# Attention and two MLPs on one core: first scatters on two queues, row tiles of 110, four buffers for evicted values, first activations split during attention

## The chip, the core and the metric

The kernel runs on one core of a Trainium2 chip. The metric is device time in microseconds (us) of one execution, as a median over several runs. Matmuls run on PE (TensorE), the other arithmetic on DVE (VectorE), ACT (ScalarE) and POOL (GpSimd). SP (SyncE) issues nearly all transfers; their packets are carried by the core's 16 DMA engines.

## The reference

Attention over 4 batches, 12 heads, 448 rows and 64 dimensions, with the heads mixed before and after the softmax; then two MLPs on the 1792 x 768 result.

```python
scores = scale * np.matmul(q, k.transpose(0, 1, 3, 2))
scores = np.einsum('bhij,hg->bgij', scores, w_pre)
scores = scores - np.max(scores, axis=-1, keepdims=True)
attn = np.exp(scores)
attn = attn / (np.sum(attn, axis=-1, keepdims=True) + 1e-09)
attn = np.einsum('bhij,hg->bgij', attn, w_post)
attn_out = np.matmul(attn, v)          # -> x: 1792 x 768
h = 1 / (1 + np.exp(-(x @ w_gate))) * (x @ w_val)    # 768 -> 1536
x = h @ w_out                                         # 1536 -> 768
h = np.maximum(x @ w_in, 0.0)                         # 768 -> 2048
out = h * h @ w_out2                                  # 2048 -> 768
```

## The kernel before

**Tiles and steps.** row_tiles (L31) cuts a batch's 448 rows into four tiles of 120, 120, 120 and 88 rows, and each tile is cut into groups of 10 rows (the last one of a batch has 8): 12, 12, 12 and 9 groups, 45 a batch, 180 in all. Two tiles make a chunk (240 and 208 columns). The loop of attention takes one group a step: premix (L182) multiplies a group's 120 (row, head) lines with the first head mixer, maximum (L190) and exponent (L198) make the softmax on DVE and ACT, normal (L209) scales the second mixer by the sums on POOL, and postmix (L224), three steps later, applies it and transposes. When a chunk's groups are through, values (L253) multiplies it by v for two heads at a time, six units a chunk.

**The scatter.** The scores of a tile come out with one row per partition, for one head at a time (L156, pairs of heads p, outputs o). ACT copies them to a buffer e (L166; DVE at L164 for the second output in the first tile), and SP scatters e into g (L170), where one partition holds one (row, head) and premix can contract over heads. If a tile of isz rows has ng whole groups and a rest, an output takes two transfers: rest partitions-groups of ng + 1 rows, and GI - rest of ng rows. A tile of 120 rows is one transfer of 10 x 12 rows of 448 floats (1792 bytes each); the tile of 88 rows is two, 8 x 9 and 2 x 8. The twelve outputs of tile n are scattered during the steps of tile n - 1: pairs p = 0 to 5, one pair a step, the last at most LA = 3 steps before the first premix of tile n, which needs all twelve. g has two buffers, e has four pairs.

**What SP's queue holds beside it.** In program order: k of the next batch (L129, one after each pair in the last tile of a batch), q of the next tile (L137), v (L243), the stores of evicted values (xs from xo, L269), and what the MLP asks for. An xo buffer is filled by ACT (L268) from PSUM; it comes from the pool pv, which has two buffers, so the third copy waits for the first store.

**The MLP beside attention.** The MLP is a generator, advanced by attention: in the last EARLY = 64 steps every third step gives it one piece ("yield 1"), and after the last scores every step two ("yield 2"); beyond the last premix three. Its list `early` there loads the first weight tiles (w_raw, 768 KB each, L422) and splits them into high and low parts over several stages. Then x_steps loads the attention output back (xr, L530) and splits it (xh on ACT, L546; xl on POOL or DVE), for chunks c of 0 and 1 (batches 0 and 1), six tiles each. Its buffers xr come from a pool of two, and the split results stand in the pool px, which is opened only after the buffers of the scores are closed. From 566 us on PE runs the MLP's matmuls alone (L612).

**Order.** The program is scheduled by hand: the order in which the loop issues instructions is the order on each engine. PE, ACT, DVE, POOL and SP each go through their own in order.

Of the kernel before, what the change touches and what calls it, by code (L numbers as in the profile page):

```python
# [7 lines left out]
F32 = mybir.dt.float32  # L8
# [8 lines left out]
P = 128  # L17
# [5 lines left out]
NA = 9  # L23
MW, PW, VW, SW, STEP = 0.76, 0.82, 1.66, 1.04, 2.55
KB = 10
EARLY = 64
EM = 2
EACH = (1, 2, 2)


def row_tiles(S):  # L31

    n = -(-S // (4 * GI)) * GI
    cuts = [t * n for t in range(4)] + [S]
    return list(zip(cuts, cuts[1:]))

# [6 lines left out]
def attention(tc, q, k, v, w_pre, w_post, xs, B, H, S, D):  # L43
# [31 lines left out]
    with ExitStack() as ctx, ExitStack() as mid, ExitStack() as left:  # L75
        kw = dict(side="right")
        one = ctx.enter_context(tc.tile_pool(name="a_one", bufs=1, **kw))
        pv = ctx.enter_context(tc.tile_pool(name="a_v", bufs=2, **kw))
        pp = ctx.enter_context(tc.tile_pool(name="a_p", bufs=1, **kw))
        pa = mid.enter_context(tc.tile_pool(name="a_a", bufs=NA, **kw))  # L80
        pg = mid.enter_context(tc.tile_pool(name="a_g", bufs=2, **kw))
# [60 lines left out]
        def scores(n, p):  # L142

            b, i0, isz = tiles[n]
            if p == 0:
                g_t[n] = pg.tile([KM, GT, S], F32, tag="g", name="g")
            kt = k_t.pop((b, p)) if i0 + isz == S else k_t[b, p]
            ps = [
                ps_b.tile([P, S], F32, tag="b", name="ps_s")
                if n == 0 and p % 2  # L150
                else ps_q.tile([P, S], F32, tag="q", name="ps_s")
                for _ in range(2)
            ]
            for o in range(2):
                r = slice(o * D, (o + 1) * D)
                nc.tensor.matmul(  # L156
                    ps[o][:isz], lhsT=q_t[n][r, p, :isz], rhs=kt[r], start=True, stop=True
                )
            e = p4.tile([IM, 2, S], F32, tag="e", name="e")
            ng, rest = divmod(isz, GI)  # L160
            to = g_t[n].rearrange("(r h) g j -> h r g j", h=H)
            for o in range(2):
                if n == 0 and o:
                    nc.vector.tensor_copy(e[:isz, o], ps[o][:isz])  # L164
                else:
                    nc.scalar.copy(e[:isz, o], ps[o][:isz])  # L166
                for r0, r1, g in ((0, rest, ng + 1), (rest, GI, ng)):
                    if r0 < r1:
                        e0 = r0 * (ng + 1)
                        nc.sync.dma_start(  # L170
                            out=to[2 * p + o, r0:r1, :g], in_=e[e0 : e0 + (r1 - r0) * g, o]
                        )


# [89 lines left out]
        def valued(c, h, ps):  # L264
            b, i0, i1 = chunks[c][:3]
            w = i1 - i0
            xo = pv.tile([P, CM], F32, tag="xo", name="xo")
            nc.scalar.copy(xo[:, :w], ps[:, :w])  # L268
            nc.sync.dma_start(out=xs[b][h * D : (h + 2) * D, i0:i1], in_=xo[:, :w])  # L269

# [41 lines left out]
            load_next(k_load, k_order)  # L312
            load_next(k_load, k_order)
        masks()
        q_load(1)
        for p in range(NP):
            scores(0, p)
        mixers()
        for _ in range(2):
            load_next(v_load, v_order)  # L320
        for _ in range(KB - NP):
            load_next(k_load, k_order)
        for s in range(NG + 30):
            if s < NG:
                premix(s)
            flush()
            if s < NG:
                maximum(s)
            if 1 <= s <= NG:
                exponent(s - 1)  # L330
            if 2 <= s < NG + 2:
                normal(s - 2)
            left_over = STEP - MW
            ready = front and front[0][0] <= s
            if ready and due(s):
                next_scores()
                ready, left_over = False, left_over - SW
            fresh = None
            while bpos < len(back) and (left_over > 0.5 or s >= NG):
                f, cost, *x = back[bpos]  # L340
                if f is postmix:
                    if x[0] > s - LAG:
                        break
                    fresh = groups[x[0]][3]
                elif x[0] == fresh:
                    if s < NG:
                        break
                    flush()
                if len(pending) > 3:
                    flush()  # L350
                f(*x)
                if f is values and (x[1] + 2) % HV == 0:
                    pending.append((load_next, v_load, v_order))
                bpos += 1
                left_over -= cost
                if f is postmix and x[0] == NG - 1:
                    flush()
                    mid.close()
                if s >= NG:
                    yield 3 if bpos == len(back) or back[bpos][0] is values else 2  # L360
            if ready and left_over > 0.4:
                next_scores()
            if not front and not closed:
                left.close()
                closed = True
            if NG - EARLY <= s < NG:
                if closed:
                    yield 2
                elif s % 3 == 0:
                    yield 1  # L370
# [3 lines left out]
def mlp(tc, xs, wg, wv, wo, wi2, wo2, out, DM, DF1, DF2):  # L374
# [12 lines left out]
    with ExitStack() as ctx:  # L387
# [5 lines left out]
        pf = pool("m_f", 2, side="left")  # L393
        p1 = pool("m_1", 1, side="left")
        pw3 = pool("m_w3", 3, side="left")
        pw = pool("m_w", 3, side="left")
        dram = pool("m_dram", 1, space=DRAM)
        yield 1

# [126 lines left out]
        xr = {}  # L526

        def x_load(hf, c, i):
            xr[c, i] = pf.tile([P, N], F32, tag="xr", name="xr")
            nc.sync.dma_start(out=xr[c, i], in_=xs[hf * NC + c][i * P : (i + 1) * P, :])  # L530

        def halves(p, tag, src):
# [8 lines left out]

        def x_split(hf, c, i):
            t = xr.pop((c, i))
            hi = px.tile([P, N], F32R, tag="xh", name="xh")
            lo = px.tile([P, N], F32R, tag="xl", name="xl")
            nc.scalar.copy(hi, t)  # L546
            (nc.vector if hf or i % 2 else nc.gpsimd).tensor_tensor(
                out=lo, in0=t, in1=hi.bitcast(F32), op=ALU.subtract
            )
            xt[c, i] = (hi, lo)  # L550

        def x_steps(hf):
            if hf * NC < NX:
                todo = [(c, i) for c in range(NC) for i in range(KD)]
                for n in range(len(todo) + 2):
                    if n >= 2:
                        x_split(hf, *todo[n - 2])
# [3 lines left out]
                        yield  # L561


        steps = x_steps(0)

        early = [0, 0, 1, 2, 0, 1, 3, 0, 2, 4, 1, 3, 2, 4, 3, 1]
        for n, k in enumerate(early):
            advance(k)
            yield 1 if n + 1 < len(early) else 2
        px = pool("m_x", KD * NC, side="left")  # L570
        for n, _ in enumerate(steps):
            if n in (4, 10):
                advance(5)
            if n in (7, 13):
                advance(6)
            if n == 8:
                advance(0)
            yield 2 if n < 14 else 3
        yield 3
        pe = pool("m_e", 3, side="left")  # L580
        ph0 = pool("m_h0", EM * NC, side="left")
# [81 lines left out]
        for hf in range(NX // NC):  # L663
# [24 lines left out]
                w_used()  # L688

            x2 = {}  # L690
            long(K1, KD, g, lambda c, m, ps: to(x2, (c, m), px, "x", ps))

            hh = {}
            while (NC - 1, KD - 1) not in x2:
# [5 lines left out]
                    product(ps, wt, x2, c, then=squared(hh, c, m, ps))  # L700
                w_used()

            todo = iter(x_steps(hf + 1))
            long(K2, KD, hh, lambda c, m, ps: store(hf, c, m, ps), todo)
            for _ in todo:
                pass
# [63 lines left out]
```

## Time and profile before

| | us |
|---|---|
| median of 3 runs | 1523.88 (1523.6 to 1529.14) |
| profiled execution, its time | 1531.59 |
| profiled execution, its span | 1529.9 |
| PE busy in the span | 1491.3 (97%), 38.6 idle |
| DVE, ACT, POOL busy | 765.1 (50%), 537.8 (35%), 508.0 (33%) |
| L612, the MLP's matmuls, at the end of the span | from 566.00, 960.35 us, 4714 of them |

PE is the engine that is nearly always busy, so the views to read are those of PE's idle time and of PE's order: what it waited for, the time from one premix to the next (a step), and which transfer or engine released it. A row of the timeline gives start and length in us, the engine (SPq is SP's queue of issues), the line, and in brackets the idle time before it with what ended it. PEclk is the clock that was granted to PE, 1.00 for 2.4 GHz and 0.50 for 1.2 GHz. The share of the DMA engines is a mean over 16.

### The profile page before, as it was taken

The page shows a single profiled execution, that of the slowest core. Times are in us where ns is not written, and L with a number is a line of the kernel's source. Part 1 is how long each engine was busy: PE and PEld are TensorE (multiplying, and loading weights), DVE is VectorE, ACT ScalarE, POOL GpSimd, SP SyncE. Part 2 cuts the span into 40 slices and gives each one's busy share as a digit, 9 for nine tenths or more (in the row PEclk, how much of TensorE's full clock was granted, in tenths as well). Part 3 has the DMA queues.
Part 4 walks back from the last instruction along what each step waited for, and adds up shares of the span by engine and source line. Part 5 has one row for each costly group of instructions (what it writes and reads, how often), then busy time and mean ns, then how long its engine had stood idle before and what let it go on. Part 6 is the DMA issues. An engine that isn't in the chain of part 4 may idle for free.

```text
span 1529.9 us, 21163 instructions
## 1 busy us (share of the span) xinstructions
PE 1491.3 (97%) x7848; PEld 1210.1 (79%) x7848; DVE 765.1 (50%) x1275; ACT 537.8 (35%) x1102; POOL 508.0 (33%) x403
## 2 busy tenths in 40 slices
PE   5999999999999899999999999999999999999999
PEld 2555656646555689999999999999999999999998
DVE  2645546546474478777889998921111101333000
ACT  3544444444344333333234443322222212333111
POOL 0222222221223346455555555532222222223221
PEclk8999999999999999999999999999999999999999
DMA  6354454445534344444444446632111111112221
GB/s 216 109 151 131 125 147 141 125 137 160 160 99 152 94 158 176 165 156 158 173 159 161 157 160 203 216 122 62 43 61 54 61 42 59 55 52 60 77 71 42
DMA packets 79531, 185.42 MB, mean 121 GB/s; under 512 B 11204, under 2 KB 48452, under 8 KB 79428
## 3 DMA queue, kind: packets, MB, share of 16 engines
q1 hardware_dynamic: 79428, 184.07, 37.5%
q8 instruction: 62, 1.02, 0.3%
q14 instruction: 41, 0.34, 0.1%
HBM read 107.75 MB, written 37.75 MB: 95 GB/s over the span
## 4 chain that ended last, share of the span: by engine, by line
PE 63%; DMA 0%; DVE 0%; POOL 0%; issue 0%; ACT 0%; ACTq 0%; DVEq 0%; SPq 0%; POOLq 0%
PE ps L612 63%; DMA w_raw<-in_wv 0%; POOL w L472 0%; POOL wl L485 0%; DVE w_t L454 0%; ACT w_f L432 0%; DVE w_f L461 0%; DVE w L441 0%; DVE w_t L438 0%; ACT o L644 0%; DVE ps L630 0%; DVEq L441 0%; ACTq L644 0%; SPq L422 0%; POOLq L472 0%
## 5 line engine op out<-in xcount | busy, mean ns | idle before, releaser
L485 POOL TENSOR_TENSOR wl<-w,wh 128x768 fp32r<-128x768 f32 (+1 forms) x140 | 259.4, 1855 | 544.7 <-ACT wh L479 538.6
L612 PE MATMUL ps<-xh,wl 128*128 128x448 f32 x960 | 351.1, 366 | 1.2 <-POOL wl L485 1.2
L612 PE MATMUL ps<-xh,wh 128*128 128x448 f32 x960 | 351.4, 366 | 0.0
L612 PE MATMUL ps<-xl,wh 128*128 128x448 f32 x960 | 351.1, 366 | 0.0
L612 PE MATMUL ps<-hl,wh 128*128 128x448 f32 x672 | 246.8, 367 | 0.0
L612 PE MATMUL ps<-hh,wl 128*128 128x448 f32 x672 | 246.8, 367 | 0.0
L612 PE MATMUL ps<-hh,wh 128*128 128x448 f32 x672 | 246.6, 367 | 0.0
L209 POOL TENSOR_SCALAR wn<-wq,sm 120x120 f32<-120x120 f32 x180 | 107.2, 596 | 386.4 <-DVE sm L207 249.7
L224 PEld LDWEIGHTS ps_p<-wn,a 120*112 120x112 f32 (+1 forms) x1440 | 164.6, 178 | 74.5 <-issue 46.4
L182 PE MATMUL ps_m<-g,wp 120*120 120x448 f32 x360 | 177.0, 574 | 22.4 <-DMA g<-e 11.9
L612 PEld LDWEIGHTS ps<-xh,wl 128*128 128x128 f32 x960 | 180.6, 188 | 16.2 <-POOL wl L485 1.8
L190 DVE TENSOR_REDUCE nm<-ps_m 120x1 f32<-120x448 f32 x180 | 112.3, 624 | 161.0 <-PE ps_m L182 152.3
L612 PEld LDWEIGHTS ps<-xh,wh 128*128 128x128 f32 x960 | 180.6, 188 | 15.4 <-issue 0.9
L612 PEld LDWEIGHTS ps<-xl,wh 128*128 128x128 f32 x960 | 180.6, 188 | 14.4
L224 PE MATMUL ps_p<-wn,a 120*112 120x120 f32 (+1 forms) x1440 | 177.4, 271 | 3.5 <-POOL wn L209 3.2
L472 POOL TENSOR_TENSOR w<-w,w_f 128x768 f32<-128x768 f32 (+1 forms) x70 | 135.3, 1933 | 60.1 <-DVE w_f L461 60.1
L236 DVE COPY ap<-ps_p 112x480 f32<-112x480 f32 x180 | 117.5, 654 | 49.8 <-PE ps_p L224 48.9
L198 ACT ACTIVATE a<-ps_m,nm 120x448 f32<-120x448 f32 x180 | 115.4, 641 | 74.7 <-DVE sm L204 63.0
L612 PEld LDWEIGHTS ps<-hh,wh 128*128 128x128 f32 x672 | 126.1, 188 | 11.7
L612 PEld LDWEIGHTS ps<-hl,wh 128*128 128x128 f32 x672 | 126.1, 188 | 11.6
L612 PEld LDWEIGHTS ps<-hh,wl 128*128 128x128 f32 x672 | 126.1, 188 | 11.6
L166 ACT COPY e<-ps_s 120x448 f32<-120x448 f32 (+1 forms) x186 | 90.0, 533 | 128.2 <-PE ps_s L156 107.9
(39 smaller groups left out, 1291.5 us busy)
## 6 DMA issues: line engine op xcount, KB each, us to landing
g<-e SPq DMA_DIRECT2D x144, 210.0 KB
ws<-w SPq DMA_DIRECT2D x58, 384.0 KB
w<-ws SPq DMA_DIRECT2D x58, 384.0 KB
w_raw<-in_wo SPq DMA_DIRECT2D x18, 768.0 KB
w_raw<-in_wi SPq DMA_DIRECT2D x16, 768.0 KB
vraw<-in_v SPq DMA_DIRECT2D x24, 448.0 KB
w_raw<-in_wg SPq DMA_DIRECT2D x12, 768.0 KB
w_raw<-in_wv SPq DMA_DIRECT2D x12, 768.0 KB
```

Of the source, the lines that this page charges most:

```text
L166: nc.scalar.copy(e[:isz, o], ps[o][:isz])
L182: nc.tensor.matmul(ps[:kk], lhsT=w[:kk, :kk], rhs=g_t[n][:kk, r0 // GI], start=True, stop=True)
L190: nc.vector.tensor_reduce(out=nm[:kk], in_=ps[:kk], op=ALU.max, axis=AX.X, negate=True)
L198: nc.scalar.activation(a[:kk], ps[:kk], AF.Exp, bias=nm[:kk], accum_out=sm[:kk])
L209: nc.gpsimd.tensor_scalar(out=wn[:kk], in0=wq[:kk], scalar1=sm[:kk], scalar2=None, op0=ALU.mult)
L224: nc.tensor.matmul(ps[:JP, jt], lhsT=a[:kk, jt * JP : (jt + 1) * JP], rhs=wn[:kk].rearrange("p g i -> p (g i)"), start=True, stop=True,)
L236: nc.vector.tensor_copy(ap[c][:, :, :, g0 - i0 : g0 - i0 + rows], ps[:JP, :, :, :rows])
L472: nc.gpsimd.tensor_tensor(out=x[:, s], in0=x[:, s], in1=fs.pop(n)[:, s], op=ALU.add)
L485: nc.gpsimd.tensor_tensor(out=lo[:, s], in0=w32.pop(n)[:, s], in1=h[:, s].bitcast(F32), op=ALU.subtract)
L612: nc.tensor.matmul(ps, lhsT=a, rhs=x, start=first and n == 0, stop=last and n == total - 1)
```

## The change

- row_tiles rounds the tile down: 110, 110, 110 and 118 rows, groups 11, 11, 11, 12 (45 a batch as before), chunks of 220 and 228 columns. An output's scatter is 10 x 11 in the first three tiles, and 8 x 12 with 2 x 11 in the last.
- In the first tile the e copies of pairs 4 and 5 go to buffers of the pool of activations, which are free at that time, and four of the twelve scatters (second outputs of pairs 1, 3, 4, 5) are issued by ACT.
- The load of q for the second tile, the first two of v and four of k are moved: q behind the first scatters, v to steps 4 and 6, k to steps 8 to 11.
- xo has a pool of its own with four buffers.
- EARLY is 112. x_steps is called for chunk 0 first, every third step from step 69 on, with three xr buffers and a px pool for chunk 0 opened at the start; the list `early` follows behind it, so that w_raw falls to steps 105, 108 and 126 (before: 117, 120 and 138). The pool of rounded weights (pw) and the px pool for chunk 1 are opened where the buffers of scores are closed, and chunk 1 is split there.

```diff
-EARLY = 64
+EARLY = 112
...
 def row_tiles(S):
 
-    n = -(-S // (4 * GI)) * GI
+    n = S // (4 * GI) * GI
...
         pv = ctx.enter_context(tc.tile_pool(name="a_v", bufs=2, **kw))
+        po = ctx.enter_context(tc.tile_pool(name="a_o", bufs=4, **kw))
...
-            e = p4.tile([IM, 2, S], F32, tag="e", name="e")
+            if n == 0 and p >= 4:
+                e = [pa.tile([IM, S], F32, tag="a", name="e0") for _ in range(2)]
+            else:
+                t = p4.tile([IM, 2, S], F32, tag="e", name="e")
+                e = [t[:, o] for o in range(2)]
...
-                    nc.scalar.copy(e[:isz, o], ps[o][:isz])
+                    nc.scalar.copy(e[o][:isz], ps[o][:isz])
+                queue = nc.scalar if n == 0 and o and p in (1, 3, 4, 5) else nc.sync
                 for r0, r1, g in ((0, rest, ng + 1), (rest, GI, ng)):
                     if r0 < r1:
                         e0 = r0 * (ng + 1)
-                        nc.sync.dma_start(
-                            out=to[2 * p + o, r0:r1, :g], in_=e[e0 : e0 + (r1 - r0) * g, o]
+                        queue.dma_start(
+                            out=to[2 * p + o, r0:r1, :g], in_=e[o][e0 : e0 + (r1 - r0) * g]
                         )
...
-            xo = pv.tile([P, CM], F32, tag="xo", name="xo")
+            xo = po.tile([P, CM], F32, tag="xo", name="xo")
...
         masks()
-        q_load(1)
         for p in range(NP):
             scores(0, p)
         mixers()
-        for _ in range(2):
-            load_next(v_load, v_order)
-        for _ in range(KB - NP):
-            load_next(k_load, k_order)
+        q_load(1)
         for s in range(NG + 30):
             if s < NG:
                 premix(s)
             flush()
             if s < NG:
                 maximum(s)
+            if s in (4, 6):
+                load_next(v_load, v_order)
+            if 8 <= s < 8 + KB - NP:
+                load_next(k_load, k_order)
...
-        pw = pool("m_w", 3, side="left")
+        px = [pool("m_x0", KD, side="left")]
+        pxr = pool("m_xr", 3, side="left")
...
-            xr[c, i] = pf.tile([P, N], F32, tag="xr", name="xr")
+            xr[c, i] = pxr.tile([P, N], F32, tag="xr", name="xr")
...
-        def x_steps(hf):
+        def x_steps(hf, chunks):
             if hf * NC < NX:
-                todo = [(c, i) for c in range(NC) for i in range(KD)]
+                todo = [(c, i) for c in chunks for i in range(KD)]
...
-        steps = x_steps(0)
+        for _ in x_steps(0, [0]):
+            yield 1
 
         early = [0, 0, 1, 2, 0, 1, 3, 0, 2, 4, 1, 3, 2, 4, 3, 1]
         for n, k in enumerate(early):
             advance(k)
             yield 1 if n + 1 < len(early) else 2
-        px = pool("m_x", KD * NC, side="left")
-        for n, _ in enumerate(steps):
-            if n in (4, 10):
+        pw = pool("m_w", 3, side="left")
+        px.append(pool("m_x1", KD, side="left"))
+        for n, _ in enumerate(x_steps(0, [1])):
+            if n in (2, 6):
                 advance(5)
-            if n in (7, 13):
+            if n in (4, 8):
                 advance(6)
-            if n == 8:
+            if n == 5:
                 advance(0)
-            yield 2 if n < 14 else 3
+            yield 2
```

SP's queue in the first batch, from the first scatter of the last tile on; g<-e are scatters, k<-in_k the loads of k. Before:

```order
L170 DMA g<-e 8x9x448
L170 DMA g<-e 2x8x448
L170 DMA g<-e 8x9x448
L170 DMA g<-e 2x8x448
L129 DMA k<-in_k 128x448
L170 DMA g<-e 8x9x448
L170 DMA g<-e 2x8x448
L170 DMA g<-e 8x9x448
L170 DMA g<-e 2x8x448
L129 DMA k<-in_k 128x448
```

After:

```order
L176 DMA g<-e 8x12x448
L176 DMA g<-e 2x11x448
L176 DMA g<-e 8x12x448
L176 DMA g<-e 2x11x448
L130 DMA k<-in_k 128x448
L176 DMA g<-e 8x12x448
L176 DMA g<-e 2x11x448
L176 DMA g<-e 8x12x448
L176 DMA g<-e 2x11x448
L130 DMA k<-in_k 128x448
```

Order and number of the transfers are as before; a pair of parts has 12 and 11 rows where it had 9 and 8.

SP's queue in the third batch, at its second weight tile. Before, the last scatters of a pair, then the first weight load with the stores of the first chunk's values right behind it, and the next:

```order
L170 DMA g<-e 8x9x448
L170 DMA g<-e 2x8x448
L422 DMA w_raw<-in_wg 128x1536
L269 DMA xs_59<-xo 128x240 x2
L243 DMA vraw<-in_v 112x1024
L269 DMA xs_59<-xo 128x240
L170 DMA g<-e 8x9x448
L170 DMA g<-e 2x8x448
L170 DMA g<-e 8x9x448
L170 DMA g<-e 2x8x448
L422 DMA w_raw<-in_wv 128x1536
L269 DMA xs_59<-xo 128x240
```

After, the same two weight loads:

```order
L275 DMA xs_58<-xo 128x228 x2
L249 DMA vraw<-in_v 112x1024
L176 DMA g<-e 10x11x448 x6
L429 DMA w_raw<-in_wg 128x1536
L176 DMA g<-e 10x11x448 x6
L138 DMA q<-in_q 128x708
L429 DMA w_raw<-in_wv 128x1536
L176 DMA g<-e 8x12x448
```

The weight loads moved out of the stores of the first chunk's values (xs_59) to between the scatters of tiles ahead of them; the stores ahead of them there are the last of the previous batch's.

PE at the end of attention, from the premix of the last but one group on; ps_p is postmix, ps_v the values, ps the MLP. Before:

```order
L182 MATMUL ps_m<-g,wp 120x448
L224 MATMUL ps_p<-wn,a 112x120 x4
L182 MATMUL ps_m<-g,wp 96x448
L224 MATMUL ps_p<-wn,a 112x120 x16
L253 MATMUL ps_v<-ap,vraw 64x208 x40
L612 MATMUL ps<-xh,wh 128x448
L612 MATMUL ps<-xl,wh 128x448
L612 MATMUL ps<-xh,wl 128x448
```

After:

```order
L188 MATMUL ps_m<-g,wp 120x448
L230 MATMUL ps_p<-wn,a 112x120 x4
L188 MATMUL ps_m<-g,wp 96x448
L230 MATMUL ps_p<-wn,a 112x120 x16
L621 MATMUL ps<-xh,wh 128x448
L621 MATMUL ps<-xl,wh 128x448
L621 MATMUL ps<-xh,wl 128x448
L621 MATMUL ps<-xh,wh 128x448
```

Five of the last chunk's six units of values stood ahead of the first MLP matmul. Now each of the first three stands behind a further block of 36 of them, and the last three behind the fourth block.

## Rows read from the trace of the kernel before

**Rows 1.** What PE waited for: us in total, times, longest.
```profile
PE ps_m L182 <- DMA g<-e: 11.9, 1, 11.9
...
PE ps_m L182 <- ACT a L198: 10.1, 4, 3.1
...
PE ps L612 <- POOL wl L485: 1.2, 1, 1.2
```

**Rows 2.** The chain that ended last, in order of time: start, us, what.
```profile
566.00 960.35 PE ps L612 x4714
```

**Rows 3.** Timeline at the start, SP's queue and PE.
```profile
6.88 0.48 SPq L137 DMA_DIRECT2D q<-in_q  x1
...
7.49 10.41 SPq L170 DMA_DIRECT2D g<-e  x12
...
22.84 1.82 PE L182 MATMUL ps_m<-g,wp 120*120 120x448 f32 x2 [11.91 <-DMA g<-e]
```

**Rows 4.** Stretch of 1 us: PE, PEld, DVE, ACT, POOL, PEclk, DMA share, GB/s.
```profile
17.00:18.00 1.00, 0.00 (x0) 0.00 (x0) 0.00 (x0) 0.00 (x0) 0.00 (x0) 0.50 0.66 244
```

**Rows 5.** Timeline of SP's queue, then of ACT, at the third batch's first values.
```profile
331.39 0.41 SPq L422 DMA_DIRECT2D w_raw<-in_wg  x1
```
```profile
339.20 0.36 ACT L268 COPY xo<-ps_v 128x240 f32<-128x240 f32 x1 [6.48 <-DMA xs<-xo]
```

**Rows 6.** Timeline of PE's premix rows around the third batch's values.
```profile
334.33 1.01 PE L182 MATMUL ps_m<-g,wp 120*120 120x448 f32 x2
...
340.24 1.01 PE L182 MATMUL ps_m<-g,wp 120*120 120x448 f32 x2 [2.20 <-ACT a L198]
...
343.87 1.01 PE L182 MATMUL ps_m<-g,wp 120*120 120x448 f32 x2
...
347.50 1.01 PE L182 MATMUL ps_m<-g,wp 120*120 120x448 f32 x2
...
352.51 1.85 PE L182 MATMUL ps_m<-g,wp 120*120 120x448 f32 x2 [2.35 <-ACT a L198]
...
356.54 0.92 PE L182 MATMUL ps_m<-g,wp 120*120 120x448 f32 x2
...
358.94 0.92 PE L182 MATMUL ps_m<-g,wp 120*120 120x448 f32 x2
...
397.88 1.01 PE L182 MATMUL ps_m<-g,wp 120*120 120x448 f32 x2
...
410.30 1.01 PE L182 MATMUL ps_m<-g,wp 120*120 120x448 f32 x2
...
413.75 1.01 PE L182 MATMUL ps_m<-g,wp 120*120 120x448 f32 x2
```

**Rows 7.** Stretches in the scatter of the first batch's last tile, columns as in Rows 4.
```profile
94.70:97.20 2.50, 2.50 (x21) 1.33 (x18) 0.50 (x3) 1.44 (x5) 0.59 (x1) 1.00 0.26 85
...
81.90:82.50 0.60, 0.60 (x5) 0.02 (x1) 0.43 (x1) 0.00 (x0) 0.58 (x1) 1.00 0.50 173
82.70:83.10 0.40, 0.40 (x2) 0.21 (x2) 0.00 (x0) 0.40 (x2) 0.00 (x0) 1.00 0.14 45
109.00:110.00 1.00, 1.00 (x7) 0.61 (x6) 0.78 (x2) 0.09 (x1) 0.30 (x1) 1.00 1.05 298
```

**Rows 8.** Timeline: first scatters of that tile on SP's queue, its first premix on PE.
```profile
80.45 2.95 SPq L170 DMA_DIRECT2D g<-e  x4
```
```profile
111.87 0.98 PE L182 MATMUL ps_m<-g,wp 120*120 120x448 f32 x2 [0.23 <-DMA q<-in_q]
```

**Rows 9.** Timeline of PE in the fourth batch, at the splits of the first activations.
```profile
485.51 1.85 PE L182 MATMUL ps_m<-g,wp 120*120 120x448 f32 x2 [3.13 <-ACT a L198]
```

**Rows 10.** Timeline of PE at the end of attention.
```profile
513.91 5.85 PE L253 MATMUL ps_v<-ap,vraw 112*64 112x208 f32 x64 [0.65 <-DVE ap L236]
522.16 2.32 PE L253 MATMUL ps_v<-ap,vraw 112*64 112x208 f32 x16 [2.40 <-DMA vraw<-in_v]
524.41 0.74 PE L612 MATMUL ps<-xh,wh 128*128 128x448 f32 x1
...
526.41 0.37 PE L612 MATMUL ps<-xh,wl 128*128 128x448 f32 x1
```

More of the change, by code (lines that the diff above doesn't have):

```diff
@@ L163, in scores @@
                 if n == 0 and o:
-                    nc.vector.tensor_copy(e[:isz, o], ps[o][:isz])
+                    nc.vector.tensor_copy(e[o][:isz], ps[o][:isz])
                 else:
-                    nc.scalar.copy(e[:isz, o], ps[o][:isz])
+                    nc.scalar.copy(e[o][:isz], ps[o][:isz])
+                queue = nc.scalar if n == 0 and o and p in (1, 3, 4, 5) else nc.sync
                 for r0, r1, g in ((0, rest, ng + 1), (rest, GI, ng)):
@@ L543, in x_split @@
             t = xr.pop((c, i))
-            hi = px.tile([P, N], F32R, tag="xh", name="xh")
-            lo = px.tile([P, N], F32R, tag="xl", name="xl")
+            hi = px[c].tile([P, N], F32R, tag="xh", name="xh")
+            lo = px[c].tile([P, N], F32R, tag="xl", name="xl")
             nc.scalar.copy(hi, t)
@@ L690, in mlp @@
             x2 = {}
-            long(K1, KD, g, lambda c, m, ps: to(x2, (c, m), px, "x", ps))
+            long(K1, KD, g, lambda c, m, ps: to(x2, (c, m), px[c], "x", ps))
             hh = {}
@@ L701, in mlp @@
                 w_used()
-            todo = iter(x_steps(hf + 1))
+            todo = iter(x_steps(hf + 1, range(NC)))
             long(K2, KD, hh, lambda c, m, ps: store(hf, c, m, ps), todo)
```

## The prediction

> **What bounds the kernel now.** I began with PE's share of the profile, since PE is busy for 97% of the span, and then asked what ended its 38.6 us of idle time. The list of waits [rows 1] shows two large entries: 11.9 us at the first premix, behind the first scatter, and 10.1 us for exponent on ACT, in four waits. The chain of waits [rows 2] shows that from 566.00 us on PE runs 4714 matmuls in 960.35 us without a gap, 0.204 us each. The change leaves these matmuls and their number alone, so all that it can move lies before 566 us: the start, the steps of attention, and the handover. There a step, from one premix to the next, is PE's own length (2.40 us for two postmixes, from 356.54 to 358.94; 3.63 us for scores and 240 columns of values, from 343.87 to 347.50; 3.45 us with 208 columns, from 410.30 to 413.75 [rows 6]), unless something is late. Both kernels have 180 steps with the same matmuls in number, so I count only what is late.
>
> All sums are differences of the profiled execution (span 1529.9 us, 1531.59 us with what lies around it), applied to the median of 1523.88 us. That execution lies 7.7 us above the median, so one part of a wait seen here may be larger than usual; this goes into the range.
>
> **Four buffers for evicted values, and weight loads earlier: 12.0 us less.** In the third batch SP issues a weight load of 768 KB at 331.39 us, and the stores of evicted values queue behind it. With two xo buffers the third copy on ACT waits 6.48 us for the first store [rows 5], exponent is queued behind that copy on ACT, and the premix on PE waits for exponent. Step by step [rows 6]: 334.33 to 340.24 takes 5.91 instead of 3.63, 2.28 too much; 347.50 to 352.51 takes 5.01 instead of 2.40, 2.61; the step behind it 4.03 instead of 2.40, 1.63, with its matmuls twice as long (the premix takes 1.85 us there, 0.92 at 356.54); and the two steps from 397.88 to 410.30 take 12.42 instead of 6.90, 5.52. The sum is 12.0 us. After the change the two weight loads stand between scatters of earlier tiles, and two more copies fit before a store must be through. One of both would do, so I take all 12.0; the low end is 8, if a weight load then delays a scatter by half of what it delayed the store.
>
> **First tile: 3.4 us less.** Twelve scatters are issued from 7.49 us on, and the premix runs at 22.84 [rows 3]; PE does nothing for 11.91 us. Near the end the share of the DMA engines is 0.66 [rows 4], which is ten of sixteen and a little: a scatter of 10 x 12 rows occupies ten engines with 12 packets of 1792 bytes each. These ten are the limit. On each lie 12 x 12 = 144 packets, and the load of q issued at 6.88 (360 KB, a sixteenth each, as much as 13 packets). After, there are 12 x 11 = 132 and no q: 25 packets less. A packet costs 0.08 us [rows 7] up to 15.35 / 157 = 0.098 us (the whole stretch), so 2.0 to 2.5 us; I take 2.2, since the stretch is one long burst. The first scatter is also issued 0.6 us earlier without the q load ahead of it, and the first loads of v no longer compete with the last two scatters, some 0.6 us (448 KB over sixteen engines are 16 packets each, half of that in front). Sum 3.4; ends 0 and 4.5. The q load lands well before it is needed at step 1's scores only if it is not last: it now stands behind the scatters, and a delay there costs up to 1 us, inside these ends.
>
> By the Trainium skill, *Trainium Kernel Development and Optimization*, section Key Constraints, transfers issued by several engines run on the same sixteen DMA engines, and issuing from a second one saves only issue time. The row on the share speaks for that rule, and by it the second queue alone would be worth nothing here.
>
> **End of attention: 6.1 us less.** Before, the values of the last chunk stand ahead of the MLP: PE waits 0.65 us for ap and 2.40 us for v, the last sixteen of them take 2.32 instead of 5.85 / 4 = 1.46 us, the first five matmuls of the MLP take 2.00 us (524.41 to 526.41) instead of 1.02 [rows 2, 10], and later it waits 1.2 us for a weight tile [rows 1]. After, 36 MLP matmuls stand between the units, 36 x 0.204 = 7.3 us a block, in which v lands and the clock is not lost, and the weights are begun 12 steps earlier. 0.65 + 2.40 + 0.86 + 0.98 + 1.2 = 6.1. Ends 3 and 7.
>
> The extra stages of the MLP that now lie inside attention (six splits on ACT and POOL) go beside PE; their cover is the idle half of ACT and two thirds of POOL. I take them at nothing, and at 2 us if that cover is gone.
>
> **Even tiles: some 31 us more.** This is the part that decides. The last tile of a batch is scattered in two parts per output. The first, 8 x 9 rows, shows a DMA share of 0.50 and 173 GB/s, the second, 2 x 8 rows, a share of 0.14 and 45 GB/s [rows 7]: eight engines, then two, one part after the other and not side by side, as if the two were among the eight. Per engine that is 21.6 and 22.5 GB/s, 0.083 and 0.080 us for a packet of 1792 bytes. So the busiest two engines carry 9 + 8 = 17 packets an output, 12 x 17 = 204 a tile; after the change 12 + 11 = 23, or 276. The 72 more cost 72 x 0.082 = 5.9 us.
>
> By the Trainium skill, *DMA: Bandwidth & Descriptors*, section Why a DMA increments its semaphore by 16 and not by 1, a transfer uses the largest number of engines up to 16 that divides the slowest dimension of both sides, and the lowest-numbered ones. The row's shares agree with the eight and the two; that the two are the same ones is shown only by their not overlapping.
>
> Before, this tile has no slack. Its scatters begin at 80.45, and its first premix at 111.87 already waited 0.23 us, for the transfers behind [rows 8]. The stretch was 31.4 us long; in it the engines stood nearly idle once, from 94.70 to 97.20 at a share of 0.26 [rows 7], 2.50 x 0.74 = 1.85 us, which the longer transfers can fill. And the stretch becomes shorter: tile 2 has 11 groups instead of 12, one step of 2.40 less, and 220 columns instead of 240 save (3.63 - 3.45) x 20 / 32 = 0.11 in each of six units, 0.7. So PE waits 5.9 + 3.1 - 1.85 = 7.1 us at this premix, and it loses clock: the step behind a wait of 2.35 us took 1.63 too long [rows 6]. That is 8.7 us a batch, in the first three batches 26.2. In the second, two loads of the first activations come on top, 8 packets an engine each, 1.3 us. In the fourth there are no k loads of a next batch, six times 8 packets or 3.9 us, so 7.1 - 3.9 = 3.2 us; they add to the wait for the splits there (3.13 us at 485.51 [rows 9]), which stays, because six loads still stand behind the last scatters. 26.2 + 1.3 + 3.2 = 30.7 us. Ends for one batch: 5.0 (0.080 us, and only the one step of 2.40, with another microsecond of idle time filled, and clock kept) and 11.6, given as a rival.
>
> **Sum.** 12.0 + 3.4 + 6.1 = 21.5 us less, 30.7 us more: 9.2 us longer, 1523.88 + 9.2 = 1533.1. I forecast 1533 us.
>
> **Rivals.**
> - *The scatter stays hidden* (faster). The share is a mean over sixteen engines; if the two engines of the second part are other ones, the busiest carry 12 packets an output instead of 9, 36 more a tile, 2.9 us, and the 14 engines without work have room; likewise if transfers that now stand in between (k, v, stores) run in the gaps. Then a wait of at most 1 us a batch is left, 4 us: 1523.88 - 21.5 + 4 = 1506. The sign turns at (21.5 - 1.3 - 3.2) / 3 = 5.7 us a batch, clock included. Against it stands that the shares follow one another and that the premix at 111.87 waited already.
> - *The two engines never rest and packets are dear* (slower still). With all sixteen busy 298 GB/s flow [rows 7], 18.6 each, 0.096 us a packet. 72 more are 6.9, nothing of the idle time is filled: 6.9 + 3.1 + 1.63 = 11.6 a batch, 34.9 in three, with 1.3 and 6.1 in the fourth 42; net 20.8, 1545. It decides from the point where the k loads queue behind the second parts on these engines.
> - *The start doesn't change* (the second queue does nothing, ten engines stay full until 22.8): 3.4 us are not gained, 1536 to 1537.
>
> **How the numbers follow.** What a measurement of this kernel can tell from no change is about 0.5%, 7.6 us: 1516.3 to 1531.5. Forecast 0.46, with its own range of 1520 to 1541 (waits of 5.0 to 9 us a batch), about half of it within the band; hidden 0.31, 1501 to 1519, nearly all below the band; dear 0.15, above it; start unchanged 0.08, mostly above it. Faster 0.27, same 0.30, slower 0.43. The range 1503 to 1545 leaves out the low end of the hidden case and the top of the dear one.
>
> **What would show it.** In the profile after: the premix of the first group of a batch's last tile waits some 7 us for g in three batches, with a step at half clock behind it, and stretches with a share near 0.13 fill the time before; no copy to xo waits for a store; the first premix comes at 19.4; the first MLP matmul follows the last postmix without a wait for v. If these premixes wait under 1 us, the price of the even tiles is wrong, and the time is near 1506.

## The result, and the profile after

The changed kernel takes 1542.23 us as a median (1540.56 to 1542.57), the kernel before 1526.51 us beside it: 1.0095 times as long, with a 95% interval of 1.0070 to 1.0119, or 11 to 18 us. The forecast was slower, 1533 us. The profiled execution has a span of 1538.8 us, 8.9 us more than the one before; the sum of the prediction, which was made against that span, said 9.2.

| stretch of the span, us | before | after | difference | forecast |
|---|---|---|---|---|
| up to the first premix | 22.84 | 22.42 | -0.42 | -3.4 |
| first batch (45 steps) | 113.09 | 119.41 | +6.32 | +8.7 |
| second batch | 120.17 | 129.75 | +9.58 | +10.0 |
| third batch | 126.25 | 126.52 | +0.27 | +8.7 - 6.5 = +2.2 |
| fourth batch, to its last premix | 124.32 | 122.83 | -1.49 | +3.2 - 5.5 = -2.3 |
| from there to the end | 1023.23 | 1017.87 | -5.36 | -6.1 |

The 12.0 us of the xo buffers are split in the last column as they fell in [rows 6], 6.5 in the third batch and 5.5 in the fourth.

What PE waited for (total, times, longest), the list that [rows 1] is taken from. The four waits for exponent that had 10.1 us are one of 6.7, and waits at premix for transfers have come in:

```profile
PE ps_m L188 <- DMA vraw<-in_v: 13.8, 2, 7.2
PE ps_m L188 <- DMA q<-in_q: 10.3, 1, 10.3
PE ps_m L188 <- ACT a L204: 6.7, 1, 6.7
PE ps_m L188 <- DMA g<-e: 4.6, 2, 3.0
```

The name in such a row is the transfer that landed last by the profile; 10.3 is the start, the 13.8 and 3.0 of the 4.6 are the first premix of the last tile in batches one, two and three. PE's timeline shows them, each with the premix behind it, the first also with the one ahead:

```profile
101.15 0.92 PE L188 MATMUL ps_m<-g,wp 120*120 120x448 f32 x2
...
110.34 1.82 PE L188 MATMUL ps_m<-g,wp 120*120 120x448 f32 x2 [6.63 <-DMA vraw<-in_v]
...
114.89 0.92 PE L188 MATMUL ps_m<-g,wp 120*120 120x448 f32 x2
...
240.13 1.82 PE L188 MATMUL ps_m<-g,wp 120*120 120x448 f32 x2 [7.21 <-DMA vraw<-in_v]
244.64 0.92 PE L188 MATMUL ps_m<-g,wp 120*120 120x448 f32 x2
...
367.03 1.67 PE L188 MATMUL ps_m<-g,wp 120*120 120x448 f32 x2 [3.03 <-DMA g<-e]
371.16 0.92 PE L188 MATMUL ps_m<-g,wp 120*120 120x448 f32 x2
```

Before, the first premix of the first batch's last tile had a wait of 0.23 us [rows 8]. Now PE stands there for 6.63 us, and its next step takes 4.55 us (110.34 to 114.89) where the same two postmixes took 2.40 [rows 6]: another 2.1 us at the lower clock. The SP queue shows where it came from. The issues of four of the six pairs in the first batch, four scatters each:

```profile
82.50 2.86 SPq L176 DMA_DIRECT2D g<-e  x4
...
88.35 3.67 SPq L176 DMA_DIRECT2D g<-e  x4
...
93.30 3.78 SPq L176 DMA_DIRECT2D g<-e  x4
...
99.32 3.97 SPq L176 DMA_DIRECT2D g<-e  x4
```

Four issues take 2.9 us in an early pair, as before (2.95 [rows 8]); now the later pairs take up to 4.0. The queue's list of waits from 76 to 113 us has eight waits of these issues for earlier scatters, 3.8 us in all; the kernel before has none from 78 to 113 us. So the transfers ahead are not through. Behind the last of these issues the DMA engines go on while PE does nothing (columns as in rows 4: PE, PEld, DVE, ACT, POOL, PEclk, DMA share, GB/s):

```profile
104.50:105.50 1.00, 0.00 (x0) 0.00 (x0) 0.00 (x0) 0.00 (x0) 0.00 (x0) 1.00 0.85 220
105.50:106.50 1.00, 0.00 (x0) 0.00 (x0) 0.00 (x0) 0.00 (x0) 0.00 (x0) 1.00 0.70 106
...
109.20:110.10 0.90, 0.00 (x0) 0.00 (x0) 0.00 (x0) 0.00 (x0) 0.00 (x0) 0.50 0.62 172
```

The forecast of a share near 0.13 ahead of the premix didn't come. SP's queue issues k, q, two stores and v there, from 103.60 to 106.95 us; that they fill the other engines, so that the mean hides two late ones, is inferred, since the trace shows no engine by number. PEclk is down to 0.50 by the end of the wait.

In the fourth batch PE waits for exponent, and exponent stands on ACT behind the copy that splits the first activations, which waits for its load behind the last scatters ([rows 9] had 3.13 us):

```profile
490.84 0.56 ACT L553 CAST xh<-xr 128x448 fp32r<-128x448 f32 x1 [8.59 <-DMA xr<-xs]
```
```profile
493.06 1.85 PE L188 MATMUL ps_m<-g,wp 120*120 120x448 f32 x2 [6.70 <-ACT a L204]
```

At the end the first MLP matmul follows the last postmix at once. Of the waits of [rows 10], 0.65 and 2.40 us, there are left 0.3 us for ap and 0.4 for v:

```profile
526.45 1.07 PE L230 MATMUL ps_p<-wn,a 96*112 96x120 f32 x8 [0.58 <-POOL wn L215]
527.28 0.45 PE L621 MATMUL ps<-xh,wh 128*128 128x448 f32 x1
```

### The profile page after: what moved, and what is told of

Same layout as the page of the kernel before. It is cut to its first block, busy times and chain, and to the rows that moved or that the text cites. A ratio compares the mean times of both kernels' runs of the same rounds, so it can differ in the third digit from the quotient of the medians.

```text
span 1538.8 us, 21140 instructions
## 1 busy us (share of the span) xinstructions
PE 1491.5 (97%) x7848; PEld 1211.4 (79%) x7848; DVE 758.5 (49%) x1275; ACT 538.3 (35%) x1102; POOL 505.9 (33%) x403
## 2 busy tenths in 40 slices
DMA packets 84395, 185.42 MB, mean 120 GB/s; under 512 B 17348, under 2 KB 54212, under 8 KB 84292
## 4 chain that ended last, share of the span: by engine, by line
PE 91%; DMA 6%; DVE 1%; POOL 1%; issue 0%; SPq 0%; ACT 0%; POOLq 0%; ACTq 0%
PE ps L621 65%; PE ps_p L230 8%; PE ps_m L188 8%; PE ps_s L157 5%; PE ps_v L259 4%; DMA g<-e 3%; DMA vraw<-in_v 1%; DMA xr<-xs 1%; DVE nm L196 1%; POOL wn L215 0%; DVE ap L242 0%; SPq L176 0%; DMA q<-in_q 0%; DMA k<-in_k 0%; DVE xl L554 0%
## 5 line engine op out<-in xcount | busy, mean ns | idle before, releaser
L230 PEld LDWEIGHTS ps_p<-wn,a 120*112 120x112 f32 (+1 forms) x1440 | 168.0, 181 | 75.9 <-issue 49.4
L188 PE MATMUL ps_m<-g,wp 120*120 120x448 f32 x360 | 177.0, 574 | 35.5 <-DMA vraw<-in_v 13.8
L230 PE MATMUL ps_p<-wn,a 120*112 120x120 f32 (+1 forms) x1440 | 180.7, 275 | 3.5 <-POOL wn L215 3.0
L171 ACT COPY e<-ps_s 110x448 f32<-110x448 f32 (+1 forms) x186 | 90.1, 535 | 127.8 <-PE ps_s L157 100.2
```

What stands on the lines that cost most here:

```text
L171: nc.scalar.copy(e[o][:isz], ps[o][:isz])
L188: nc.tensor.matmul(ps[:kk], lhsT=w[:kk, :kk], rhs=g_t[n][:kk, r0 // GI], start=True, stop=True)
L230: nc.tensor.matmul(ps[:JP, jt], lhsT=a[:kk, jt * JP : (jt + 1) * JP], rhs=wn[:kk].rearrange("p g i -> p (g i)"), start=True, stop=True,)
```

## The experiments

Times are medians; the ratio is to the kernel before beside it, with its 95% interval, and is taken over all runs, so that it is not the quotient of two medians. Three groups each shared a chip: x1 to x4, x5 to x9, and y1 to y3. Across the groups only the ratios compare.

| kernel | us | ratio | interval |
|---|---|---|---|
| changed | 1542.23 | 1.0095 | 1.0070 to 1.0119 |
| x1, changed with old tiles | 1522.09 | 0.9969 | 0.9955 to 0.9982 |
| x2, before with tiles of 110 | 1544.17 | 1.0107 | 1.0087 to 1.0127 |
| x3, changed, last tile cut 10 x 11 + 8 x 1 | 1519.65 | 0.9956 | 0.9938 to 0.9973 |
| x4, before, last tile cut 10 x 8 + 8 x 1 | 1523.68 | 0.9976 | 0.9961 to 0.9991 |
| x5, before with four xo buffers | 1521.94 | 0.9945 | 0.9925 to 0.9964 |
| x6, x1 with one queue | 1522.22 | 0.9948 | 0.9929 to 0.9967 |
| x7, before with the MLP's part alone | 1527.49 | 0.9990 | 0.9975 to 1.0004 |
| x9, x3 with whole lines of q | 1522.26 | 0.9959 | 0.9942 to 0.9976 |
| y1, x6 with the cut | 1519.61 | 0.9948 | 0.9929 to 0.9967 |
| y2, y1 with EARLY = 106 | 1511.41 | 0.9896 | 0.9875 to 0.9917 |
| y3, x3 with one queue, EARLY = 106 | 1518.23 | 0.9934 | 0.9914 to 0.9955 |

**Are the tiles the price?** The theory: the last tile's two-part scatter loads two engines. The rivals: the loads that moved into attention, the smaller pieces of q, or the 118 rows as such. x1 takes the tiles out of the change (its edit is below), x2 puts them alone into the kernel before.

```diff
-    n = S // (4 * GI) * GI
+    n = -(-S // (4 * GI)) * GI
```

> The changed kernel with row_tiles rounded up again (120, 120, 120, 88), all else as changed. If the even tiles are what costs, their price is read from the steps of the two traces by batch (6.3, 9.6, 0.3 + 6.5 and -1.5 + 5.5, some 27 us), and this kernel comes to 1542 - 27 = 1515 us, its waits at the first premix of a batch's last tile under 1 us. If the waits come from the loads of activations and weights that now lie inside attention, the tiles make no difference and it stays at 1538 to 1542.

> The kernel before with row_tiles rounded down alone (110, 110, 110, 118). If the even tiles cost the 27 us by themselves, 1526 + 27 = 1553 us, with 6 to 8 us of waiting at the first premix of the last tile in each of the first three batches. If they cost only beside the earlier loads of activations, it stays within 8 us of 1526.

The tiles cost some 19 us in the changed kernel (1.0095 against 0.9969; 20 by medians) and 16 us in the kernel before. Both are less than the 27 that was expected. In x1 the first premix of the last tile waits at most 0.3 us in the first three batches, as expected; by batch the trace of the changed kernel is 7.8, 8.7, -1.1 and 3.3 us longer than that of x1. In the third batch the old tiles have a wait of their own, of which more below.

x2's waits are not those that were expected. Instead of 6 to 8 us at the first premix of the last tile it has 1.23, 2.23 and 2.70 us in the first three batches, and PE waits more for exponent, 15.1 us where the kernel before has 10.1:

```profile
PE ps_m L182 <- ACT a L198: 15.1, 7, 5.1
```
```profile
110.59 0.98 PE L182 MATMUL ps_m<-g,wp 120*120 120x448 f32 x2 [1.23 <-DMA vraw<-in_v]
```

With two xo buffers, part of the price shows at the copies to xo: on ACT they wait 29.7 us for stores, in nine waits, where the kernel before has 19.8 in four. The sign is settled, the mechanism not yet.

**Is it the two engines?** x3 keeps tiles, bytes and the number of transfers, and only cuts the last tile's scatter in another way: all whole groups as one transfer, the last group of eight rows as a second (q is laid out to match).

```diff
-                for r0, r1, g in ((0, rest, ng + 1), (rest, GI, ng)):
-                    if r0 < r1:
-                        e0 = r0 * (ng + 1)
+                for rows, g0, g1 in ((GI, 0, ng), (rest, ng, ng + 1)):
+                    if rows:
+                        z = g0 * GI
...
-                            out=to[2 * p + o, r0:r1, :g], in_=e[o][e0 : e0 + (r1 - r0) * g]
+                            out=to[2 * p + o, :rows, g0:g1], in_=e[o][z : z + rows * (g1 - g0)]
```

> The changed kernel with its tiles of 110 and 118, but the last tile's scatter cut another way: all whole groups as one transfer of 10 x 11 rows, the last group of 8 rows as a second one of 8 x 1. The bytes and the number of transfers are the same; the busiest engine carries 12 packets an output where it carried 23. If the two engines of the second part set the end, the waits of 7 us at the first premix of the last tile fall under 1 us and the time to 1515 to 1522. If the cause is the load of q, which with tiles of 110 is made of pieces of 440 bytes where it was whole lines, or the tile's 34% more rows as such, the waits stay at 5 us and more and the time at 1535 to 1542.

> The kernel before with the same cut: 10 x 8 and 8 x 1 where it had 8 x 9 and 2 x 8, 9 packets on the busiest engine where it had 17. If the last tile had no slack, as the wait of 0.23 us at 111.87 said, but lost hardly anything there, 1522 to 1526: the small gaps at that tile go (0.7 us a batch), and the splits of the first activations in the fourth batch are begun up to 3 us earlier. If these two engines already cost the kernel before some us in most executions (its runs differ by 9 us), it falls to 1515 to 1521.

x3 takes 1519.65 us, 21 to 23 less than the changed kernel (by ratio and by medians), as the theory said. The moved loads, the pieces of q and the 118 rows are all still in x3, so none of these rivals makes that price by itself. Its first premix of the last tile, in the first and the second batch:

```profile
104.74 0.98 PE L189 MATMUL ps_m<-g,wp 120*120 120x448 f32 x2 [0.43 <-issue]
...
227.29 0.98 PE L189 MATMUL ps_m<-g,wp 120*120 120x448 f32 x2 [2.51 <-DMA k<-in_k]
```

6.63 us became 0.43, and no step at half clock follows; 7.21 became 2.51, not under 1 as expected. Two loads of activations lie in the same stretch, for which the prediction had 1.3 us. In the kernel before, the same cut (x4) gives 1 to 6 us, and not at the last tile's first premix: in the first two batches, where [rows 8] has its 0.23 us, x4's trace is 0.2 us shorter and 0.6 longer. It is 5.5 and 3.6 us shorter in the third and fourth, and ACT's copies to xo wait 14.5 us for stores instead of 19.8. With four xo buffers and the old tiles, the cut gave nothing that could be measured (x6 and y1 below, both 0.9948).

x9 loads q of a tile as one line per partition, instead of six pieces of 440 bytes, which the tiles of 110 had brought in (the changed kernel moves 17348 packets under 512 bytes, the one before 11204).

```diff
-                q_t[n] = p2.tile([P, NP, IM], F32, tag="q", name="q")
+                t = p2.tile([P, NP * IM], F32, tag="q", name="q")
+                q_t[n] = t[:, : NP * isz].rearrange("d (p i) -> d p i", p=NP)
...
```

> The changed kernel with the last tile's scatter cut as 10 x 11 and 8 x 1, and q of a tile loaded into one line of 660 floats per partition instead of six pieces of 440 bytes. If the pieces (768 a load) cost engine time beside the scatters, the first premix comes at 20.5 to 21.5 instead of 22.2 us, the waits that are left at the tiles (2.5 us in the second batch) shrink by half, and the time falls by 2 to 5 us under its twin's 1519.7. If their cost is nothing, the time stays within 1 us of it.

No gain is to be seen: 0.9959 against 0.9956, the first premix at 22.20 against 22.15 us, and a wait of 3.17 us in the second batch where x3 has 2.51. The intervals leave room for a gain of some 3 us, so the upper part of the expected 2 to 5 is out and the lower part is not.

**Where did the gains go?** x1 has all of the change but the tiles, for which the prediction had 21.5 us, and gains 3 to 7 us. So three parts were tried apart.

> The kernel before with a pool of four buffers for xo, and nothing else. The sum of the prediction says that either the buffers or the earlier weight loads take away the 12.0 us of the third and fourth batch's values: then 1528 - 12 = 1516 us, and no copy to xo waits for a store over 1 us. If the weight loads then hold up the scatter that is queued behind them on the same engines, half of it comes back at the first premix of the last tile in the third batch: 1520 to 1523.

```diff
+        po = ctx.enter_context(tc.tile_pool(name="a_o", bufs=4, **kw))
...
-            xo = pv.tile([P, CM], F32, tag="xo", name="xo")
+            xo = po.tile([P, CM], F32, tag="xo", name="xo")
```

Four buffers alone are worth 0.55%, 8.4 us (5.5 to 11.5; 6.6 by medians). In the trace the third batch is 4.5 us shorter and the fourth 6.3, 10.8 of the 12.0; ACT's list of waits has no copy to xo behind a store, where 19.8 us stood before. Of the 12.0, the first premix of the third batch's last tile takes some back: it waits 1.66 us for g at 356.46 us, less than the half that was named as the other case. The step that took 5.91 us in [rows 6] has its own length, with the weight load still ahead of the stores; two rows of x5:

```profile
336.46 1.01 PE L183 MATMUL ps_m<-g,wp 120*120 120x448 f32 x2
340.09 1.01 PE L183 MATMUL ps_m<-g,wp 120*120 120x448 f32 x2
```

> The kernel before with the MLP's part of the change alone: the list of early steps from step 69 on, chunk 0 split first, weight loads at steps 105, 108 and 126; two xo buffers as before, tiles of 120 and 88. If the earlier weight loads alone free the stores, the 12.0 us go here too, and the end of attention gives 6; against that stands the wait of 4.93 us at step 114 that the changed kernel with old tiles shows, with its half clock 6.5 us: 1528 - 12 - 6 + 6.5 = 1517 us. If two xo buffers still wait for stores behind the loads of activations, 1522 to 1526.

The MLP's part alone is worth nothing measurable, and 1527.49 us is above both expectations. Its trace gives 6.0 us at the end of attention and 6.0 in the fourth batch, and takes 2.4 in the third, 3.6 in the second, 1.1 in the first, and a start that comes 1.2 later in this execution. In the third and fourth batch PE no longer waits behind the stores (ACT still does, 10.8 us in five waits), so for PE the weight loads' new place does there what four buffers do. But in the first two batches the first premix of the last tile now waits 1.52 and 2.15 us, and there is the new wait at step 114, 5.98 us here. It is in x1 as well, where SP's queue and PE show it:

```profile
301.14 0.50 SPq L429 DMA_DIRECT2D w_raw<-in_wg  x1
302.15 7.01 SPq L176 DMA_DIRECT2D g<-e  x6
309.21 0.49 SPq L429 DMA_DIRECT2D w_raw<-in_wv  x1
310.26 4.31 SPq L176 DMA_DIRECT2D g<-e  x4
```
```profile
323.47 1.82 PE L188 MATMUL ps_m<-g,wp 120*120 120x448 f32 x2 [4.93 <-DMA g<-e]
```

The two weight loads, taken out from ahead of the stores, now lie between the scatters of the third tile, and these land late. y2 moves them by six steps, behind the last of those scatters, and changes nothing else against y1:

```diff
-EARLY = 112
+EARLY = 106
```

> The changed kernel with tiles of 120, 120, 120, 88, the last one scattered as 10 x 8 and 8 x 1, and all first scatters on SP. If the cut is worth as much here as in the kernel before (4 us), 1522 - 4 = 1518 us. If the last tile of 88 rows has slack enough once PE is not late elsewhere, no gain: 1521 to 1523. The wait at step 114 (5 us, with its half clock 6.5) stays by both.

> The same with EARLY = 106, which puts the two weight loads behind the last scatter of the third batch's third tile (steps 111 and 114 instead of 105 and 108). If these two loads, 768 KB each, are what the premix of step 114 waits for, that wait goes below 1 us and the time falls by 5 to 6.5 us under its twin. If the scatter of that tile is late by itself, the wait stays and the time too. If the loads now hold up the last tile, 2 to 4 us come back at step 126.

y1 stands at 0.9948 like x6, which it differs from by the cut: with the old tiles and four xo buffers the cut gave no gain. y2 is 8.2 us faster than y1 (1519.61 to 1511.41; 4 to 12 by the two intervals), where 5 to 6.5 were expected. The premix of step 114 in y1, then in y2:

```profile
323.81 1.82 PE L189 MATMUL ps_m<-g,wp 120*120 120x448 f32 x2 [5.84 <-DMA g<-e]
```
```profile
317.83 0.98 PE L189 MATMUL ps_m<-g,wp 120*120 120x448 f32 x2 [0.50 <-DMA q<-in_q]
```

In these two profiles y2's third batch is 7.0 us shorter, and no wait over 0.3 us comes back at step 126; but the stretch from the last premix to the end is 3.0 us longer (1020.10 against 1017.12), nearly all of it in the last 4752 matmuls of the MLP. So the six steps are not free; the two profiled executions differ by 4.5 us in all, less than the medians. y2 is faster than both kernels, by 1.0% than the one before. It keeps the old tiles, with the last one cut 10 x 8 and 8 x 1, and one queue, and takes from the change the moved loads of q, v and k, the four xo buffers and the order of the MLP's part, begun six steps later.

**Does the second queue do anything?** x6 is x1 with all first scatters on SP.

```diff
-                queue = nc.scalar if n == 0 and o and p in (1, 3, 4, 5) else nc.sync
+                queue = nc.sync
```

> The changed kernel with old tiles and all twelve first scatters issued by SP. Its two-queue twin shows the first premix at 23.99 us where the kernel before has 22.84. If ten full engines set the end and two queues only mix the transfers, so that all of them land late, the first premix comes at 21.5 to 22.5 here, 1.5 to 2.5 us earlier than the twin, 1520 us in all. If issuing is what limits (0.86 us a scatter, 12 of them), it comes at 24 or later and the time is 1522 or more.

Two queues are not faster: the ratio is 0.9969 with two (x1) and 0.9948 with one (x6), a difference of 3.2 us, about as large as its error. First premix in x1, then in x6:

```profile
23.99 1.82 PE L188 MATMUL ps_m<-g,wp 120*120 120x448 f32 x2 [12.06 <-DMA g<-e]
```
```profile
21.95 1.82 PE L188 MATMUL ps_m<-g,wp 120*120 120x448 f32 x2 [10.91 <-DMA q<-in_q]
```

One execution each, and the start differs from one to the next: it came at 22.15 to 23.99 us in the four profiles with two queues, at 21.95 to 22.76 in the four with one queue and the q load moved, and at 22.80 to 24.85 in the five with the old order. That x6 begins 2 us before its twin was expected (1.5 to 2.5), but the four with two queues differ by 1.8 us among themselves, so it isn't shown that two queues make the scatters land later. A gain by the second queue is not to be seen.

**Are even tiles good once they are cut well?**

> The even tiles with the cut of 10 x 11 and 8 x 1, one queue, EARLY = 106. If even tiles cost only by the two engines of the last tile's second part, this kernel is level with the 88-row one beside it, within 3 us. If the last tile of 118 rows stays the tightest place (34% more bytes in a stretch three steps shorter), it is 4 to 8 us slower.

y3 is 6.8 us slower than y2 with the same rest (1 to 10 by the two intervals): 118 rows stay the tighter last tile. The first premix of that tile waits 0.98, 1.76 and 1.04 us in the first three batches, and PE waits 5.11 us at the splits of the fourth. In y2 that premix has no wait over 0.3 us; the scores behind it wait 0.36 and 0.83 us for q in the first two batches, and the splits cost 2.28.

## Why the prediction came out as it did, step by step

**Even tiles (forecast 30.7 us more): right in mechanism, too dear by a third.** x3 shows that the cut of the last tile's scatter is the cause; that it acts by two engines of the eight fits the count of packets. The wait was forecast as 7.1 us, and measured 6.63 and 7.21 in the first two batches; the step at half clock as 1.63, measured 2.1. The first batch is still only 6.32 us longer, not 8.7: the kernel before lost some 1.7 us there itself (steps of 2.68, 2.79 and 3.35 us at 26.37, 109.08 and 111.87, where the changed kernel's have 2.06, 2.40 and 2.69), which the term left out but for 0.23; the rest of that gap is not traced. The larger miss is the third batch, a wait of 3.03 instead of 7.1. The prediction took the k loads out of the fourth batch only. But ten k buffers run ahead, so in the third batch two of six are left to load, as SP's queue there shows:

```profile
335.53 2.88 SPq L176 DMA_DIRECT2D g<-e  x4
338.52 0.36 SPq L130 DMA_DIRECT2D k<-in_k  x1
338.98 2.86 SPq L176 DMA_DIRECT2D g<-e  x4
341.94 0.37 SPq L130 DMA_DIRECT2D k<-in_k  x1
342.41 2.86 SPq L176 DMA_DIRECT2D g<-e  x4
...
348.39 3.01 SPq L176 DMA_DIRECT2D g<-e  x4
```

Four loads fewer are 2.6 us by the prediction's own 0.65 a load, of a difference of 3.6 to 4.2; that this is all of it was counted, not tried. In the fourth batch 3.2 on top of 3.13 was forecast, 6.3, and 6.70 measured. By ratios and by medians the tiles cost 19 to 20 us (changed against x1), and the cut gave 21 to 23 (changed against x3).

**xo (forecast 12.0 less): 8.4 by x5, and the weight loads' new place was costed wrongly.** The sum of [rows 6] was of one execution that may have had longer waits than most: its time, 1531.59, lies 5 us over the median of the result. The larger error is that the sum put the weight loads between scatters at nothing; the prediction named the scatter that they might delay, at 4 us and only as an end of the range. With the old tiles their place cost 8.2 us (y1 against y2), about what the buffers gave. In the changed kernel itself less of it shows, a wait of 1.58 us at 332.15; there the second load stands behind the third tile's scatters and the q load, not between them. That this is the reason was read from the queue, not tried.

**Start (forecast 3.4 less): not gained.** All parts of the change together gave 0.4 us between the two profiles, and 0.9 between the mean of the four with two queues (22.7) and of the five with the old order (23.6), with single profiles 1.8 and 2.0 us apart in these groups. The 25 packets that were counted off an engine did not show, and x2, which takes off twelve of them, begins where the kernel before does (22.80 and 22.84); why the packets that are left take as long is open. By the Trainium skill, *Trainium Kernel Development and Optimization*, section Key Constraints, a second issuer saves only issue time; x1 against x6 agrees (ratios of 0.9969 with two issuers and 0.9948 with one).

**End of attention (forecast 6.1 less): right.** 5.4 us in the changed kernel, 6.0 in x7, 6.1 in x1.

**The sum.** 9.2 us against the profile of before, where 8.9 were measured, is closer than its terms were, and that is luck: by the table the first batch's loss came out 2.4 us smaller and the start's gain 3.0 us smaller than forecast, and the rest nearly cancels too; by the experiments losses were set too high by about a third and gains too high by more, 21.5 for what x1 shows as 3 to 7. Applied to the median the sum came out 9 us short. Of these, 6.8 are that the profiled execution of before was a long one of its kind and that of after a short one (1531.59 against a median of 1526.51, 1540.56 against 1542.23); 2.6 are the median of before, which was 1523.88 when the forecast was made. Of the rivals, the hidden scatter is refuted by the waits of 6.63 and 7.21 us, and the dear packets, which wanted 10 us, by the same rows; the unchanged start came true beside the forecast.

By the Trainium skill, *DMA: Bandwidth & Descriptors*, section Why a DMA increments its semaphore by 16 and not by 1, a transfer from SP that is spread over k of the core's sixteen engines uses the lowest-numbered k, by which the two engines of an output's second part are among the eight of its first. The trace shows no engine by number; that x3's cut, 12 packets where there were 23 if the rule holds, takes the wait away agrees with it.

## What to carry to other kernels

Before the shape of a strided transfer is changed, work out on how many DMA engines each of its parts lies and how many packets the busiest one carries: here 34% more rows in the last tile became 35% more packets on the two engines that the sum took for the busiest, with hardly any slack, and another cut of the same bytes gave 21 to 23 us back. A mean DMA share of 0.62 to 0.85 while PE waited did not show it; in the first batch the growing length of the issues did (2.9 to 4.0 us), in the third it hardly did (2.9 to 3.1). And a large load that is moved out of one wait must be followed to the next transfer with a due time behind it: six steps more were worth 8 us. The same price can also show in another place: with two xo buffers part of it stood at the stores, with four at the premix.

## What the runs showed that I had not expected

Two queues feeding ten full engines did not begin the first premix earlier: 22.2 to 24.0 us with two, 22.0 to 22.8 with one. 10 x 11 rows instead of 10 x 12 gave no shorter start either (22.80 in x2, 22.84 before), and 440-byte pieces in twelve loads of q cost nothing that could be measured (x9, to within some 3 us). The kernel before spreads from 1521.7 to 1533.6 us on the chips used, more than most of the parts tried here, so one profile of it can be some us off in its waits.
